# Last batch of a fused attention and mixture kernel: GpSimd in written order, w2's blocks in other buffers, one low part on VectorE

## The chip, the cores and the metric

The kernel runs on one core of one Trainium2 chip. The metric is device time in microseconds (us) of one execution, the median of several runs. Engines: PE is TensorE, DVE is VectorE, ACT is ScalarE, POOL is GpSimd, SP is SyncE, which here only issues DMAs.

## The reference, cut to what matters

Attention over 4 batches of 768 rows, 8 heads of 64; its output x, 3072 rows of 512, goes through four experts, all of which every row uses, weighted by its probabilities:

```python
p = domain_probs / (domain_probs.sum(-1, keepdims=True) + 1e-09)
out = np.zeros((N, D), dtype=np.float32)              # N = 3072, D = 512
for e in range(E):                                    # E = 4, F = 1024
    h = np.maximum(x @ w1[e], 0.0)
    out += p[:, e:e + 1] * (h @ w2[e])
```

## The kernel before

All is float32. To use TensorE's faster fp32r type without its error, an operand is split into a high part (the value rounded to fp32r, a copy by ScalarE or a cast by GpSimd) and a low part (value minus high part), and a product is three matmuls: high times high, low times high, high times low.

Batches 0 to 2 are interleaved with the attention of the next batch; the change leaves them alone. The last batch (`last_batch`) has no attention beside it. Its 16 units (4 experts, 4 groups of 256 hidden channels) are taken two by two, in eight stages j = 0 to 7. Both matrix products are done by a seven-product scheme for 2 by 2 blocks (Strassen's, in Winograd's form), so seven block products stand for eight.

In a unit (`small`), the seven products of w1's blocks with x's blocks (B11, T1, T2, B21, T3, T4, B22) are each 6 matmuls of 128x384, about 1.04 us. TensorE's order in a unit: A11·B11, S1·T1, S2·T2, A12·B21, S3·T3, A22·T4, S4·B22. S4·B22 is added onto the PSUM bank of S1·T1, so it can only begin when VectorE has read that bank (`ve.tensor_add(h22, pc[:, :HALF], u3)`, in the trace `hB<-pm,vv`). VectorE applies relu and the expert's share, which gives the hidden blocks `hb` B11, B22, B21, B12 (in the order they come).

At the end of a stage `sums` makes T3, T2, T1, T4 of the stage's hidden blocks on VectorE, and `form` splits all seven into `form` tiles, high part by ScalarE. The low parts of B11, B22 and B21 are GpSimd's (`po`), those of T3, T2, T1, T4 VectorE's.

In the next stage the seven big products (`big`, n = 0 to 6: A11·B11, A12·B21, S4·B22, S3·T3, S2·T2, S1·T1, A22·T4, each 12 matmuls, about 2.08 us) multiply these with the blocks of w2, in three places of the first unit and four of the second, the last of them (n = 6) just before S4·B22 of the second unit.

w2's blocks: A11, A12 and A22 come split from DRAM (`kept`). S1 to S4 are sums, made new in each stage: `ask_raw` loads 1 MB of w2 into one tile (named `x` in the trace, since it lies in the pool of that name), `sum_raw` makes the four sums in place on GpSimd (`x<-x`, four operations), and `ask` lets GpSimd cast each (high) and subtract (low) into a block buffer. That tile exists once: the next load waits until the last low part has been read from it, and the sums wait for the load.

Buffers: `wp` has two `w2s` tiles, each of two blocks, `L.w2f` three of one block. Before, one `w2s` holds A11 and A12, the other S4 and S3; S2, S1 and A22 take the `w2f` tiles. The last stage (j = 7) makes plain hidden parts instead of `form` tiles; for it `load_w2` loads two whole w2 tiles (1 MB each) into the two `w2s` buffers, and a last product for t = 0 to 5 ends the kernel.

What sets the order: each engine runs one queue in the order the scheduler wrote. In the last batch nothing is held in program order, so the scheduler may move instructions on every engine. DMAs of SP stand in one queue: one whose buffer is not free holds up those behind it.

Of the kernel before, what the change touches and what calls it, by code (L numbers as in the profile page):

```python
# [10 lines left out]
F32R = mybir.dt.float32r  # L11
# [3 lines left out]
ALU = mybir.AluOpType  # L15
# [3 lines left out]
P = 128  # L19
# [6 lines left out]
def f32(ap):  # L26
    return ap.bitcast(F32)
# [159 lines left out]
def attn_moe_kernel(ctx: ExitStack, tc, q, k, v, n_global, n_local, domain_probs, w1, w2, out):  # L187
# [19 lines left out]
    ve, ac, po, sy, te = (Ordered(tc, e) for e in (nc.vector, nc.scalar, nc.gpsimd, nc.sync, nc.tensor))  # L207
# [62 lines left out]
    wp = main.enter_context(tc.tile_pool(name="wp", bufs=2))  # L270
# [485 lines left out]
    kept, waiting = {}, {}  # L756
# [209 lines left out]
    def last_batch(L):  # L966

        b = LAST
        hb = {n: L.hb.tile([P, 2, HALF], F32, name=f"h{n}") for n in ("B11", "B12", "B21", "B22")}
        made, acc, share, w2f = {}, {}, {}, {}  # L970

        def form(name, src, low):
            t = made[name] = L.form.tile([P, 2, 2, HALF], F32R, name="form")
            ac.copy(t[:, 0], src)
            low.tensor_tensor(t[:, 1], src, f32(t[:, 0]), op=ALU.subtract)

        def sums():
            t3 = L.hb.tile([P, 2, HALF], F32, name="hT3")
# [9 lines left out]
        ORDER2 = (("A11", "B11"), ("A12", "B21"), ("S4", "B22"), ("S3", "T3"), ("S2", "T2"), ("S1", "T1"), ("A22", "T4"))  # L988
# [5 lines left out]
        a11, a21, a12, a22 = (raw[:, :, f, m] for f in range(2) for m in range(2))  # L994
        value = {"S1": a22, "S2": a11, "S3": a21, "S4": a12}

        def ask_raw(j):
            if j < per // 2 - 1:
                e, g = divmod(j, NPR // 2)
                for u in range(2):  # L1000
                    rows = w2[e, (2 * g + u) * 2 * P : (2 * g + u + 1) * 2 * P, :]
                    sy.dma_start(
                        raw[:, u].rearrange("p f m c -> p f (m c)"), rows.rearrange("(f p) m -> p f m", p=P)
                    )

        def sum_raw(j):
            if j < per // 2 - 1:
                po.tensor_add(a22, a21, a22)
                po.tensor_sub(a21, a11, a21)
                po.tensor_sub(a11, a22, a11)  # L1010
                po.tensor_sub(a12, a12, a11)

        def ask(j, n):
            if j >= per // 2 - 1:
                return
            e, g = divmod(j, NPR // 2)
            a = ORDER2[n][0]
            if n < 4:
                if n % 2 == 0:
                    w2f[(j, n // 2)] = wp.tile([P, 2, 2, 2, 2 * P], F32R, name="w2s")  # L1020
                t = w2f[(j, a)] = w2f[(j, n // 2)][:, n % 2]
            else:
                t = w2f[(j, a)] = L.w2f.tile([P, 2, 2, 2 * P], F32R, name="w2f")
            if a in value:
                po.tensor_copy(t[:, :, 0], value[a])
                po.tensor_tensor(t[:, :, 1], value[a], f32(t[:, :, 0]), op=ALU.subtract)
                if n == 5:
                    ask_raw(j + 1)
            else:
                f, m = {"A11": (0, 0), "A12": (1, 0), "A22": (1, 1)}[a]  # L1030
                for u in range(2):
                    block = kept[(e, 2 * g + u, 2)][:, :, f, m * 2 * P : (m + 1) * 2 * P]
                    sy.dma_start(f32(t[:, u]), f32(block))

        def big(j, n):
            a, x = ORDER2[n]
            pm = L.pq.tile([P, 2, 512], F32, name="pq")
            w, t = w2f[(j, a)], made[x]
            for m in range(2):
                at = 0  # L1040
                for u in range(2):
                    for wi, xi in ((0, 0), (1, 0), (0, 1)):
                        te.matmul(
                            pm[:, m, :HALF], w[:, u, wi, m * P : (m + 1) * P], t[:, xi, u, :],
                            start=(at == 0), stop=(at == 5),
                        )
                        at += 1
            if j == 0:
                acc[x] = L.acc.tile([P, 2, HALF], F32, name=f"sum{x}")
                ac.copy(acc[x], pm[:, :, :HALF])  # L1050
            else:
                ve.tensor_add(acc[x], pm[:, :, :HALF], acc[x])
            if n > 3:
                ask(j + 1, n)
            elif n % 2 == 1:
                ask(j + 1, n - 1)
                ask(j + 1, n)

        def small(i, more, plain=None):

            u = i % 2

            def out(name, f, c, src):
                if plain is None:
                    ve.scalar_tensor_tensor(
                        hb[name][:, u], src, 0.0, share[i][:, c * HALF : (c + 1) * HALF], op0=ALU.max, op1=ALU.mult
                    )
                else:
                    h = plain[f]
                    ac.activation(h[:, 0, c], src, AF.Relu)  # L1070
                    ve.scalar_tensor_tensor(h[:, 1, c], src, 0.0, f32(h[:, 0, c]), op0=ALU.max, op1=ALU.subtract)

            keep(i, 1)
            pa = product(i, "A11", "B11")
            p1 = up1.tile([P, HALF], F32, name="p1")
            ac.copy(p1, pa[:, :HALF])
            yield
            pc = product(i, "S1", "T1")
            yield
            more()  # L1080
            product(i, "S2", "T2", pm=pa, onto=True)
            u2 = up.tile([P, HALF], F32, name="u")
            ac.copy(u2, pa[:, :HALF])
            yield
            pd = product(i, "A12", "B21")
            ve.tensor_add(pd[:, :HALF], pd[:, :HALF], p1)
            out("B11", 0, 0, pd[:, :HALF])
            if u == 1 and plain is None:
                form("B11", hb["B11"], po)
            yield  # L1090
            more()
            product(i, "S3", "T3", pm=pa, onto=True)
            u3 = up.tile([P, HALF], F32, name="vv")
            ac.copy(u3, pa[:, :HALF])
            yield
            h22 = hb["B22"][:, u]
            ve.tensor_add(h22, pc[:, :HALF], u3)
            out("B22", 1, 1, h22)
            if u == 1 and plain is None:
                form("B22", hb["B22"], po)  # L1100
            more()
            product(i, "A22", "T4", pm=pa, onto=True)
            out("B21", 1, 0, pa[:, :HALF])
            if u == 1 and plain is None:
                form("B21", hb["B21"], po)
            yield
            if u == 1:
                more()
            product(i, "S4", "B22", pm=pc, onto=True)
            ve.tensor_add(pc[:, :HALF], pc[:, :HALF], u2)  # L1110
            out("B12", 0, 1, pc[:, :HALF])
            yield

        final = {}
        for j in range(per // 2):
            e, g = divmod(j, NPR // 2)
            if g == 0:
                pb = L.share.tile([P, S], F32, name="share")
                sy.dma_start(
                    pb.rearrange("p (t c) -> p t c", c=P),  # L1120
                    shares["all"][b * NQT : (b + 1) * NQT, e].partition_broadcast(P),
                )
            at = [0]

            def more():
                if j > 0:
                    big(j - 1, at[0])
                    at[0] += 1

            if j == 0:  # L1130
                ask_raw(0)
                sum_raw(0)
                for n in range(7):
                    ask(0, n)
            for i in (b * per + 2 * j, b * per + 2 * j + 1):
                share[i] = pb
                plain = None
                if j == per // 2 - 1:
                    plain = final[i] = [L.form.tile([P, 2, 2, HALF], F32R, name="form") for _ in range(2)]
                chores.append(load_w1(i + 2))  # L1140
                if j == per // 2 - 1:
                    chores.append(load_w2(i))
                for _ in small(i, more, plain):
                    work_chores()
                    yield
            if j < per // 2 - 1:
                sums()
                sum_raw(j + 1)


        for to, other in (("T2", "B11"), ("T3", "T2"), ("B21", "B11"), ("T4", "T3"), ("T2", "T1"), ("B22", "T2"), ("T1", "T3")):
# [45 lines left out]
    def work_chores():  # L1197
        for c in list(chores):
            if next(c, 0) == 0:
                chores.remove(c)  # L1200
# [49 lines left out]
    op = early.enter_context(tc.tile_pool(name="op", bufs=1))  # L1250
# [14 lines left out]
    per = E * NPR  # L1265
# [34 lines left out]
    L = Pools(main, "last", dict(form=7, acc=1, w2f=3, hb=1, share=2), dict(pq=2))  # L1300
    for _ in last_batch(L):
        pass
# [34 lines left out]
```

## Time and profile before

| | us |
|---|---|
| median of 3 runs | 1233.14 (1231.83 to 1234.08) |
| the profiled execution, its own time | 1231.64 |
| its span, first to last instruction | 1229.9 |
| busy in the span: PE, DVE, ACT, POOL | 1174.1, 842.3, 516.2, 339.5 |

Times below are from the span's start; the last batch begins at about 942. A line of the timeline gives start, length, engine, operation, output<-inputs, how many were merged, and in brackets the engine's idle time before it and who ended it. The seven forms of hidden blocks all are `form`, hidden blocks all `hB`. A digit of the granted clock in 40 slices is that of 30.7 us, in tenths of full speed.

### The profile page before, as it was taken

Reading aid. Unit: us, or ns where it says so; the run is one execution under the profiler, and the core shown is the slowest. Engines: PE = TensorE matmul, PEld = TensorE weight load, DVE = VectorE, ACT = ScalarE, POOL = GpSimd, SP = SyncE. Lnnn points to the kernel's source line nnn. Section 1 sums busy time; section 2 is a strip of 40 time slices with the busy share of each in tenths; the row PEclk is TensorE's granted clock in tenths of the full one; section 3 lists DMA queues with packets and bytes.
Section 4 is the critical chain, followed back from the end, with each engine's and each line's share of the span. In section 5 each row is a group of like instructions: output and inputs, shape, how many; then the busy total and the mean of one; then the engine's idle time right before and its main releaser. Section 6 shows DMA issues by size and latency. Waiting matters only on the chain.

```text
span 1229.9 us, 18538 instructions
## 1 busy us (share of the span) xinstructions
PE 1174.1 (95%) x6849; PEld 1066.7 (87%) x6849; DVE 842.3 (68%) x1699; ACT 516.2 (42%) x1296; POOL 339.5 (28%) x317
## 2 busy tenths in 40 slices
PE   8989999999999999999999999999999598888898
PEld 6778888889889989989989998998988498888897
DVE  6977676666677676677677757666757457777774
ACT  5735656555533434354432434444432242222231
POOL 5744736363620000000010000000003565555530
PEclk8999999999999999999999999999999799999999
DMA  9377787886988875867658666766545465455541
GB/s 194 66 240 233 258 257 256 274 280 208 338 310 249 258 222 168 246 195 204 206 180 282 208 191 210 199 221 199 175 175 197 156 213 173 149 200 205 205 146 54
DMA packets 162722, 258.29 MB, mean 210 GB/s; under 512 B 109024, under 2 KB 131136, under 8 KB 148032
## 3 DMA queue, kind: packets, MB, share of 16 engines
q1 hardware_dynamic: 159024, 250.74, 64.5%
q10 hardware_dynamic: 3600, 6.29, 1.4%
q8 instruction: 56, 0.92, 0.3%
q14 instruction: 42, 0.34, 0.1%
HBM read 185.65 MB, written 52.48 MB: 194 GB/s over the span
## 4 chain that ended last, share of the span: by engine, by line
PE 78%; DVE 8%; DMA 6%; POOL 4%; issue 2%; ACT 2%; SPq 1%; POOLq 0%; DVEq 0%; ACTq 0%
PE pm L42 62%; PE pt L42 6%; PE pq L42 6%; PE ps L42 4%; DVE form L42 2%; DMA raw<-in_moe_w_dram 2%; DVE hB L42 2%; DMA qd<-st_q 1%; DMA x<-in_moe_w_dram 1%; POOL w1s L42 1%; DVE pm L42 1%; DMA w1s<-kept 1%; POOL sums L42 1%; POOL w2f L42 1%; SPq L42 1%
## 5 line engine op out<-in xcount | busy, mean ns | idle before, releaser
L42 PE MATMUL pm<-w2s,h 128*128 128x512 f32 x1728 | 418.0, 394 | 3.2 <-DVE h L42 3.2
L42 PEld LDWEIGHTS pm<-w2s,h 128*128 128x128 f32 x1728 | 318.2, 188 | 70.3 <-DVE h L42 5.3
L42 PE MATMUL pm<-xT,w1s 128*128 128x384 f32 x1536 | 304.6, 339 | 4.0 <-DVE h L42 1.1
L42 DVE SCALAR_TENSOR_TENSOR acc<-pm,prob,acc 128x512 f32<-128x512 f32 x270 | 200.7, 748 | 114.1 <-PE pm L42 112.3
L42 PEld LDWEIGHTS pm<-xT,w1s 128*128 128x128 f32 x1536 | 268.0, 189 | 8.1 <-DVE h L42 2.2
L42 PE MATMUL pm<-xB,w1s 128*128 128x384 f32 x1152 | 235.1, 347 | 18.2 <-DVE hB L42 18.2
L42 PEld LDWEIGHTS pm<-xB,w1s 128*128 128x128 f32 x1152 | 207.4, 194 | 23.2 <-DVE hB L42 20.0
L42 POOL TENSOR_TENSOR xT<-x,xT 128x768 fp32r<-128x768 f32 x3 | 5.6, 1856 | 577.8 <-ACT xT L42 577.8
L42 ACT ACTIVATE h<-pm 128x384 fp32r<-128x384 f32 x192 | 92.3, 490 | 91.8 <-DVE pm L42 87.2
L42 ACT ACTIVATE pb<-pb,nmax 128x256 f32<-128x256 f32 (+1 forms) x192 | 92.9, 486 | 85.6 <-DVE nmax L42 85.0
L42 DVE SCALAR_TENSOR_TENSOR h<-pm,h 128x384 fp32r<-128x384 f32 x192 | 104.9, 551 | 12.1 <-ACT h L42 10.0
L42 ACT COPY p<-pm 128x384 f32<-128x384 f32 x64 | 30.5, 477 | 192.4 <-PE pm L42 175.5
L42 PE MATMUL pq<-form,w2s 128*128 128x384 f32 x336 | 64.3, 339 | 14.2 <-POOL form L42 14.2
L42 PEld LDWEIGHTS pq<-form,w2s 128*128 128x128 f32 x336 | 59.7, 191 | 14.6 <-POOL form L42 14.6
L42 ACT ACTIVATE pb<-pb,zsum 128x256 f32<-128x256 f32 (+1 forms) x144 | 63.0, 484 | 22.2 <-DVE zsum L42 22.1
L42 ACT COPY pT<-pt 128x512 f32<-128x512 f32 (+2 forms) x73 | 39.9, 547 | 49.0 <-PE pt L42 48.6
L42 DVE CUSTOM_DVE_ANT_0 pb<-ps,nbias 128x256 f32<-128x256 f32 (+1 forms) x144 | 52.9, 395 | 9.6 <-PE pt L42 6.0
L42 DVE TENSOR_TENSOR u<-pm,p 128x384 f32<-128x384 f32 x48 | 26.7, 556 | 46.9 <-PE pm L42 35.3
L42 POOL TENSOR_TENSOR x<-x 128x512 f32<-128x512 f32 x28 | 45.1, 1612 | 43.3 <-DMA x<-in_moe_w_dram 41.7
L42 PE MATMUL pt<-ident,pb 128*128 128x128 f32 x352 | 55.0, 277 | 1.7 <-DVE pT L42 1.0
L42 POOL TENSOR_TENSOR w2s<-raw,w2s 128x512 fp32r<-128x512 f32 x32 | 41.7, 1320 | 50.7 <-ACT w2s L42 50.6
L42 DVE TENSOR_TENSOR pm<-pm,vv 128x384 f32<-128x384 f32 x96 | 53.7, 559 | 2.7 <-PE pm L42 2.4
(146 smaller groups left out, 1461.2 us busy)
## 6 DMA issues: line engine op xcount, KB each, us to landing
w1s<-kept SPq DMA_DIRECT2D x48, 1792.0 KB, 7.8
w2s<-kept SPq DMA_DIRECT2D x34, 1024.0 KB, 5.1
kept<-w1s SPq DMA_DIRECT2D x16, 1792.0 KB, 10.0
qd<-st_q SPq DMA_DIRECT2D x96, 192.0 KB, 4.0
raw<-in_moe_w_dram SPq DMA_DIRECT2D x32, 512.0 KB, 6.0
kept<-w2s SPq DMA_DIRECT2D x16, 1024.0 KB, 8.2
w2s<-kept SPq DMA_DIRECT2D x28, 256.0 KB, 4.5
x<-in_moe_w_dram SPq DMA_DIRECT2D x14, 512.0 KB, 4.7
```

The source lines that it names most:

```text
L42: ins = fn(*args, **kwargs)
```

## The change

Three things, all in `last_batch`. GpSimd's instructions (sums, casts, low parts) are given to `keep_in_program_order`, so that the scheduler leaves them in the order of the program, and that order is changed: the sums of stage j's raw tile now stand in the first unit of stage j, behind its A12·B21, no longer at the end of the stage before, and each block is asked for after its own big product. The blocks share buffers otherwise: one `w2s` has A11 and A12 as before, the other S1 and A22; S4, S3 and S2 take the three `w2f` tiles. The raw tile of the next stage is asked for behind the last of the seven (n = 6). The low part of B21 goes from GpSimd to VectorE.

```diff
+            if low is po:
+                keeping(ins)
...
-                po.tensor_add(a22, a21, a22)
+                keeping(po.tensor_add(a22, a21, a22))
...
         def ask(j, n):
-            if j >= per // 2 - 1:
+
+            if j >= per // 2 - 1 or n in (0, 5):
                 return
             e, g = divmod(j, NPR // 2)
-            a = ORDER2[n][0]
-            if n < 4:
-                if n % 2 == 0:
-                    w2f[(j, n // 2)] = wp.tile([P, 2, 2, 2, 2 * P], F32R, name="w2s")
-                t = w2f[(j, a)] = w2f[(j, n // 2)][:, n % 2]
+            names = {1: ("A11", "A12"), 2: ("S4",), 3: ("S3",), 4: ("S2",), 6: ("S1", "A22")}[n]
+            if len(names) == 2:
+                t = wp.tile([P, 2, 2, 2, 2 * P], F32R, name="w2s")
             else:
-                t = w2f[(j, a)] = L.w2f.tile([P, 2, 2, 2 * P], F32R, name="w2f")
...
+                    keeping(po.tensor_copy(to[:, :, 0], value[a]))
+                    keeping(po.tensor_tensor(to[:, :, 1], value[a], f32(to[:, :, 0]), op=ALU.subtract))
...
+            if n == 6:
+                ask_raw(j + 1)
...
-            if n > 3:
-                ask(j + 1, n)
-            elif n % 2 == 1:
-                ask(j + 1, n - 1)
-                ask(j + 1, n)
+            ask(j + 1, n)
...
             out("B11", 0, 0, pd[:, :HALF])
+            if u == 0 and i > b * per:
+                sum_raw((i - b * per) // 2)
...
-                form("B21", hb["B21"], po)
+                form("B21", hb["B21"], ve)
...
                 sums()
-                sum_raw(j + 1)
```

The first place: GpSimd's queue where the last batch begins. `x_9982` is the raw tile; `w2s_9996` and the tiles numbered near it are stage 0's blocks. Before:

```order
L42 TENSOR_TENSOR w2f_10004<-x_9982,w2f_10004 128x2x256
L42 TENSOR_TENSOR x_9982<-x_9982 128x2x256 x4
L42 TENSOR_TENSOR form_10107<-hB11_9978,form_10107 128x768
L42 TENSOR_TENSOR form_10120<-hB22_9981,form_10120 128x768
L42 TENSOR_TENSOR form_10130<-hB21_9980,form_10130 128x768
L42 CAST w2s_10305<-x_9982 128x2x256 x2
```

Now:

```order
L42 TENSOR_TENSOR w2s_10005<-x_9982,w2s_10005 128x2x256
L42 TENSOR_TENSOR form_10107<-hB11_9978,form_10107 128x768
L42 TENSOR_TENSOR form_10120<-hB22_9981,form_10120 128x768
L42 TENSOR_TENSOR x_9982<-x_9982 128x2x256 x4
L42 CAST w2f_10257<-x_9982 128x2x256
```

The low parts of stage 0's hidden B11 and B22 moved ahead of the four sums of stage 1's raw tile; that of B21 left this queue.

The second place: the end of stage 2 and the change to stage 3, one period of what repeats. GpSimd before (`w2f_10618` is S2, `w2f_10648` S1):

```order
L42 CAST w2f_10618<-x_9982 128x2x256
L42 TENSOR_TENSOR form_10601<-hB11_9978,form_10601 128x768
L42 TENSOR_TENSOR w2f_10618<-x_9982,w2f_10618 128x2x256
L42 CAST w2f_10648<-x_9982 128x2x256
L42 TENSOR_TENSOR form_10631<-hB22_9981,form_10631 128x768
L42 TENSOR_TENSOR w2f_10648<-x_9982,w2f_10648 128x2x256
L42 TENSOR_TENSOR form_10660<-hB21_9980,form_10660 128x768
L42 TENSOR_TENSOR x_9982<-x_9982 128x2x256 x4
```

Now (`w2f_10619` is S2, `w2s_10673` S1 and A22):

```order
L42 TENSOR_TENSOR form_10602<-hB11_9978,form_10602 128x768
L42 CAST w2f_10619<-x_9982 128x2x256
L42 TENSOR_TENSOR w2f_10619<-x_9982,w2f_10619 128x2x256
L42 TENSOR_TENSOR form_10632<-hB22_9981,form_10632 128x768
L42 CAST w2s_10673<-x_9982 128x2x256
L42 TENSOR_TENSOR w2s_10673<-x_9982,w2s_10673 128x2x256
L42 TENSOR_TENSOR x_9982<-x_9982 128x2x256 x4
```

The cast of S1 moved behind the low part of B22 and now writes a buffer that big product n = 6 of the stage reads; the low part of B21 left the queue, so nothing stands between S1's low part and the sums of the next raw tile.

The same change of stage in SP's queue, before (`w1s` are w1's blocks for the unit after next, `w2f_10677` is A22):

```order
L42 DMA x_9982<-in_moe_w2_dram 128x2x512 x2
L42 DMA w1s_10556<-kept_1_3_1_2385 128x3584
L42 DMA w2f_10677<-kept_1_0_2_2124 128x2x256
L42 DMA w2f_10677<-kept_1_1_2_2298 128x2x256
L42 DMA w2s_10772<-kept_1_2_2_2524 128x2x256
```

Now:

```order
L42 DMA w2s_10673<-kept_1_0_2_2124 128x2x256
L42 DMA w2s_10673<-kept_1_1_2_2298 128x2x256
L42 DMA w1s_10559<-kept_1_3_1_2385 128x3584
L42 DMA x_9982<-in_moe_w2_dram 128x2x512 x2
L42 DMA w2s_10772<-kept_1_2_2_2524 128x2x256
```

The raw load went from ahead of A22 and of a `w1s` load to behind both.

The third place: TensorE's last products, where `w2s_11794` and `w2s_11902` are the two whole w2 tiles. Before:

```order
L42 MATMUL pq_11990<-form_11780,w2f_11755 128x384 x12
L42 MATMUL pm_11904<-xB22_9829,w1s_11636 128x384 x6
L42 MATMUL pm_12021<-w2s_11794,form_11783 128x512 x3
L42 MATMUL pm_12021<-w2s_11794,form_11784 128x512 x3
L42 MATMUL pm_12021<-w2s_11902,form_11891 128x512 x3
```

Now:

```order
L42 MATMUL pq_11990<-form_11780,w2s_11753 128x384 x12
L42 MATMUL pm_11904<-xB22_9829,w1s_11639 128x384 x6
L42 MATMUL pm_12021<-w2s_11794,form_11783 128x512 x3
L42 MATMUL pm_12021<-w2s_11794,form_11784 128x512 x3
L42 MATMUL pm_12034<-w2s_11794,form_11783 128x512 x3
L42 MATMUL pm_12034<-w2s_11794,form_11784 128x512 x3
L42 MATMUL pq_12047<-ident_58,sumB21_10225 128x128 x2
L42 MATMUL pq_12047<-ident_58,sumT4_10400 128x128 x2
L42 MATMUL pq_12053<-ident_58,sumB21_10225 128x128 x2
L42 MATMUL pq_12053<-ident_58,sumT4_10400 128x128 x2
L42 MATMUL pm_12063<-w2s_11794,form_11783 128x512 x2
L42 MATMUL pm_12021<-w2s_11902,form_11891 128x512 x3
```

Twelve matmuls on the first tile, eight transposes and two matmuls more now stand ahead of the first use of `w2s_11902`; before, only six matmuls did.

## Rows read from the trace of the kernel before

**Rows 1.** The page: busy time by engine, and the granted TensorE clock in 40 slices.

```profile
PE 1174.1 (95%) x6849; PEld 1066.7 (87%) x6849; DVE 842.3 (68%) x1699; ACT 516.2 (42%) x1296; POOL 339.5 (28%) x317
...
PEclk8999999999999999999999999999999799999999
```

**Rows 2.** Who TensorE waited for, from 930 to the end: total us, times, longest.

```profile
PE pm L42 <- DVE hB L42: 18.2, 5, 3.8
PE pq L42 <- POOL form L42: 14.2, 1, 14.2
```

**Rows 3.** Timeline of TensorE where stage 1 begins (big n = 0, A11·B11, then S2·T2).

```profile
957.38 0.51 PE L42 MATMUL pq<-form,w2s 128*128 128x384 f32 x2
972.14 2.61 PE L42 MATMUL pq<-form,w2s 128*128 128x384 f32 x7 [14.25 <-POOL form L42]
974.55 1.89 PE L42 MATMUL pm<-xB,w1s 128*128 128x384 f32 x6
...
977.86 1.20 PE L42 MATMUL pm<-xT,w1s 128*128 128x384 f32 x6
```

**Rows 4.** Timeline of GpSimd in the same place.

```profile
946.58 4.23 POOL L42 TENSOR_TENSOR x<-x 128x512 f32<-128x512 f32 x3 [18.26 <-DMA x<-in_moe_w_dram]
...
958.44 1.26 POOL L42 TENSOR_TENSOR w2f<-x,w2f 128x512 fp32r<-128x512 f32 x1
965.05 5.28 POOL L42 TENSOR_TENSOR x<-x 128x512 f32<-128x512 f32 x4 [5.35 <-DMA x<-in_moe_w_dram]
970.29 6.07 POOL L42 TENSOR_TENSOR form<-hB,form 128x768 fp32r<-128x768 f32 x3
```

**Rows 5.** The chain of waits: start, length, what. Where stage 1 begins, the first of two w1s loads issued behind the raw load, to its landing; near the end, the eight transposes of the first two output tiles.

```profile
960.72 8.48 DMA w1s<-kept
...
1210.55 0.87 PE pq L42 x8
```

**Rows 6.** Timeline of TensorE: the change from stage 2 to stage 3 (big n = 6, then S4·B22 with stage 3's A11·B11), and the restarts of the first unit's S4·B22 after the waits in stage 3 and in stage 6 (the second and the last of five).

```profile
1034.23 2.24 PE L42 MATMUL pq<-form,w2f 128*128 128x384 f32 x12
1036.31 2.24 PE L42 MATMUL pm<-xB,w1s 128*128 128x384 f32 x12
...
1053.81 3.65 PE L42 MATMUL pm<-xB,w1s 128*128 128x384 f32 x12 [3.81 <-DVE hB L42]
...
1157.49 3.66 PE L42 MATMUL pm<-xB,w1s 128*128 128x384 f32 x12 [3.68 <-DVE hB L42]
```

**Rows 7.** Timeline of TensorE in stage 7, which has no raw tile: S4·B22 of stage 6 with A11·B11; A22·T4 and S4·B22 of the first unit; S4·B22 of the second; the last product.

```profile
1174.51 2.24 PE L42 MATMUL pm<-xB,w1s 128*128 128x384 f32 x12
...
1186.99 1.21 PE L42 MATMUL pm<-xT,w1s 128*128 128x384 f32 x6
1188.12 2.38 PE L42 MATMUL pm<-xB,w1s 128*128 128x384 f32 x12
...
1203.86 1.20 PE L42 MATMUL pm<-xB,w1s 128*128 128x384 f32 x6
1204.90 5.65 PE L42 MATMUL pm<-w2s,form 128*128 128x512 f32 x24
```

**Rows 8.** Timeline of VectorE at the change to stage 3: the last sum of big products, the hidden block B12 from PSUM, T3, the low parts of T2, T1 and T4, and the add that reads the bank of S1·T1.

```profile
1036.51 0.96 DVE L42 TENSOR_TENSOR sumT<-pq,sumT 128x768 f32<-128x768 f32 x1 [1.52 <-PE pq L42]
...
1038.15 0.56 DVE L42 SCALAR_TENSOR_TENSOR hB<-pm,share 128x384 f32<-128x384 f32 x1
1038.74 1.79 DVE L42 TENSOR_TENSOR hT<-hB,hB 128x768 f32<-128x768 f32 x1
...
1045.54 5.96 DVE L42 TENSOR_TENSOR form<-hB,form 128x768 fp32r<-128x768 f32 x3
...
1053.21 0.54 DVE L42 TENSOR_TENSOR hB<-pm,vv 128x384 f32<-128x384 f32 x1
```

**Rows 9.** Timeline of VectorE at the change to stage 7: the same three low parts and the same add.

```profile
1183.12 2.69 DVE L42 TENSOR_TENSOR form<-hB,form 128x768 fp32r<-128x768 f32 x3
...
1187.52 0.55 DVE L42 TENSOR_TENSOR hB<-pm,vv 128x384 f32<-128x384 f32 x1
```

**Rows 10.** Timeline of GpSimd at the change to stage 3: cast S1, low B22, low S1, low B21, sums.

```profile
1034.24 0.60 POOL L42 CAST w2f<-x 128x512 fp32r<-128x512 f32 x1
1034.82 1.84 POOL L42 TENSOR_TENSOR form<-hB,form 128x768 fp32r<-128x768 f32 x1
1036.62 1.29 POOL L42 TENSOR_TENSOR w2f<-x,w2f 128x512 fp32r<-128x512 f32 x1
1037.88 1.84 POOL L42 TENSOR_TENSOR form<-hB,form 128x768 fp32r<-128x768 f32 x1
1043.50 7.18 POOL L42 TENSOR_TENSOR x<-x 128x512 f32<-128x512 f32 x4 [3.78 <-DMA x<-in_moe_w_dram]
```

**Rows 11.** Timeline of ScalarE in the same place: the high part of B21.

```profile
1035.02 0.84 ACT L42 CAST form<-hB 128x768 fp32r<-128x768 f32 x1 [0.96 <-DVE hB L42]
```

**Rows 12.** DMA issues in short windows, KB each and median us from issue to landing: the raw load issued at 1037.94, the w1s load issued behind it at 1038.92, a w1s load issued alone at 1055.57.

```profile
x<-in_moe_w_dram SPq DMA_DIRECT2D x2, 512.0 KB, 4.5
...
w1s<-kept SPq DMA_DIRECT2D x1, 1792.0 KB, 8.8
...
w1s<-kept SPq DMA_DIRECT2D x1, 1792.0 KB, 7.4
```

**Rows 13.** The two loads of whole w2 tiles in stage 7, issued at 1184.1 and 1193.7, with nothing but each other on the queue for the second.

```profile
DMA to landing us min/median/max: 5.0/5.8/6.6
```

More of the change, by code (lines that the diff above doesn't have):

```diff
@@ L970, in last_batch @@
         made, acc, share, w2f = {}, {}, {}, {}
+        keeping = tc.keep_in_program_order
         def form(name, src, low):
@@ L974, in form @@
             ac.copy(t[:, 0], src)
-            low.tensor_tensor(t[:, 1], src, f32(t[:, 0]), op=ALU.subtract)
+            ins = low.tensor_tensor(t[:, 1], src, f32(t[:, 0]), op=ALU.subtract)
+            if low is po:
+                keeping(ins)
         def sums():
@@ L1007, in sum_raw @@
             if j < per // 2 - 1:
-                po.tensor_add(a22, a21, a22)
-                po.tensor_sub(a21, a11, a21)
-                po.tensor_sub(a11, a22, a11)
-                po.tensor_sub(a12, a12, a11)
+                keeping(po.tensor_add(a22, a21, a22))
+                keeping(po.tensor_sub(a21, a11, a21))
+                keeping(po.tensor_sub(a11, a22, a11))
+                keeping(po.tensor_sub(a12, a12, a11))
         def ask(j, n):
-            if j >= per // 2 - 1:
+            if j >= per // 2 - 1 or n in (0, 5):
@@ L1015, in ask @@
                 return
             e, g = divmod(j, NPR // 2)
-            a = ORDER2[n][0]
-            if n < 4:
-                if n % 2 == 0:
-                    w2f[(j, n // 2)] = wp.tile([P, 2, 2, 2, 2 * P], F32R, name="w2s")
-                t = w2f[(j, a)] = w2f[(j, n // 2)][:, n % 2]
-            else:
-                t = w2f[(j, a)] = L.w2f.tile([P, 2, 2, 2 * P], F32R, name="w2f")
[L1024 to L1033, printed above, removed]
+            names = {1: ("A11", "A12"), 2: ("S4",), 3: ("S3",), 4: ("S2",), 6: ("S1", "A22")}[n]
@@ new lines, in ask @@
+            if len(names) == 2:
+                t = wp.tile([P, 2, 2, 2, 2 * P], F32R, name="w2s")
+            else:
+                t = L.w2f.tile([P, 1, 2, 2, 2 * P], F32R, name="w2f")
+            for at, a in enumerate(names):
+                to = w2f[(j, a)] = t[:, at]
+                if a in value:
+                    keeping(po.tensor_copy(to[:, :, 0], value[a]))
+                    keeping(po.tensor_tensor(to[:, :, 1], value[a], f32(to[:, :, 0]), op=ALU.subtract))
+                else:
+                    f, m = {"A11": (0, 0), "A12": (1, 0), "A22": (1, 1)}[a]
+                    for u in range(2):
+                        block = kept[(e, 2 * g + u, 2)][:, :, f, m * 2 * P : (m + 1) * 2 * P]
+                        sy.dma_start(f32(to[:, u]), f32(block))
```

## The prediction

> **What bounds the kernel now.** I read the page first. TensorE is busy 95% of the span, so only its idle time and its slow clock can be won; one slice of 40 has a granted clock of 0.7, the one where the last batch begins [rows 1]. Then the view of who waited for whom, over the last batch: TensorE waits for little more than two things, once 14.2 us for a low part of GpSimd and five times, 18.2 us in all, for a hidden block of VectorE [rows 2]. The timelines tell why.
>
> The long wait: big product n = 0 of stage 1 issues two matmuls at 957.4 and goes on at 972.14 [rows 3]. It needs the low part of B11. GpSimd is done with stage 0's blocks at 959.70, but next in its queue are the sums of stage 1's raw tile, whose load has not landed; they run from 965.05, and the low part comes from 970.29 to about 972.1 [rows 4].
>
> The five short waits, here in stage 3: count from T0, the end of S4·B22 that closes a stage. Rows 6 put it at 1037.35 (half of the twelve matmuls from 1036.31; twelve take 36.31 - 34.23 = 2.08 us, one 0.173). TensorE next waits from T0+12.65 to T0+16.46 for the add that reads the bank of S1·T1 [rows 6]. VectorE makes that add from T0+15.86 [rows 8], late because its three low parts took 5.96 us and T3 1.79. While they ran, GpSimd did the sums (7.18 us from 1043.50) and the low part of B21 (to 1039.72) [rows 10]. Stage 7 shows it without sums: the three low parts take 2.69, the add comes at T0+11.97 with T0 = 1175.55, and S4·B22 follows 0.1 us behind A22·T4 [rows 7, 9]. So the wait is there when GpSimd's sums lie on VectorE's low parts, and nearly gone when not.
>
> What a wait costs with its slow restart: from the restart in stage 3 to that in stage 6 are three periods, (1157.49 - 1053.81)/3 = 34.56 us [rows 6]. Stage 7, from S4·B22 to S4·B22, takes 1203.86 - 1174.51 = 29.35 [rows 7]. The difference is 5.21 a stage, 3.64 of it the idle time, the rest the restart: its twelve matmuls take 3.65 us [rows 6] where they take 2.24 otherwise [rows 7].
>
> **The written order at the start.** GpSimd's work up to 959.70 is the same (four sums, four casts, four low parts); the low part of B11 now follows it at once, 959.7 to 961.6 or, if VectorE's new low part of B21 comes between, about 1 us later. Big n = 0 then goes on some 10.5 us sooner. But what is late next is w1's blocks for A11·B11: their load stands in SP's queue behind the raw load, which waits for GpSimd's last low part both before and now; it is issued at 960.72 and lands 8.48 us later, at 969.2 [rows 5]. So A11·B11 starts at about 969.25 in place of 974.55 [rows 3], 5.3 sooner. Both runs restart slowly there: before, the nine matmuls of big n = 0 bore most of it, now A11·B11 and S1·T1 do. From 972.14 to 977.86 TensorE did 7 + 6 + 6 + 3 = 22 matmuls in 5.72 us against 3.81 at 0.173; the 15 behind A11·B11's start would need 2.6 + 1.9 = 4.5, so S2·T2 starts at 973.75 in place of 977.86: **4.1 us** won. Bounds: nothing, if the queue moves for another reason; 10.5 plus 1.9, if w1's blocks came in time.
>
> **The buffers and the raw load.** The load still waits for the low part of S1, but S1's cast now waits until big n = 6 has been read, T0-1.04. Cast 0.60 and low part 1.29 [rows 10] end at T0+0.9, and the load is issued at T0+1.0 to T0+1.6, against T0+0.6 before (1037.94) [rows 12]. In SP's queue it is now behind A22 and behind a w1s load issued at about T0+0.2. This decides whether the sums still lie on VectorE's low parts, which end at T0+10.26 in stage 7 (1183.12 + 2.69) [rows 9]. The lower bound is 4.5 us from issue as now [rows 12]: T0+5.6. The upper is w1s alone, 7.4, and the full 4.5 behind it: T0+12.1. I take the upper half: a w1s load with the raw load ahead lands 8.8 after issue, 1.4 later than alone although it was issued 1.0 later [rows 12], so loads of this queue share little and pass one after another, and the raw tile's own transfer is about 2.4 us. That gives T0+7.6+2.4 = T0+10.0, and A22's 0.5 MB ahead adds up to 1.2. The sums then run from T0+10 to T0+11 on, beside adds that read PSUM, which GpSimd does not hold up: B12's operation of 0.56 at 1038.15 lies wholly beside the low part of B21 [rows 8, 10].
>
> The five waits are gone with that: 5 x 5.21 = **26.0 us**, of which the small wait of stage 7 is kept in, since 29.35 includes it. Later sums harm nobody: from T0+16 GpSimd has the casts and low parts of S4 and S3 (1.9 each) to do before the low part of B11, whose product ends at T0+19.8 (eleven of 1.04, four of 2.08) and which TensorE needs at T0+31.
>
> **B21's low part on VectorE** adds 0.95 us (an operation of its size in rows 8 takes 0.96) seven times. Its high part ends at 1035.86, T0-1.5 [rows 11], and VectorE is idle for 1.52 us up to 1036.51 [rows 8], so most of it lies in idle time. What follows it on VectorE is the last sum, the add for B12, B12 and then T3. T3 took 1.79 beside GpSimd's low part of B21, which is gone, and 0.83 with it. The bounds: 0.83 won, if B21's stays in the gap; 2.1 lost a stage, if GpSimd's low B22, cast S1 and low S1 each go ahead of it: then it runs T0+1.2 to T0+2.2, behind it 0.96 + 0.6 + 0.6 + 0.96 for sum, add, B12 and T3, which ends at T0+5.3 in place of T0+3.18. I take a delay of about 0.5, which the shorter T3 pays, and 0.1 a stage for what is left: **-0.5 us**.
>
> Here the profile shows that T3 with 0.98 us of GpSimd's low part beside it takes 0.83 longer than an operation of its size [rows 8, 10]. The Trainium skill, page "SBUF — State Buffer", section "Who interferes with whom", says that a VectorE instruction with two SBUF inputs and a GpSimd instruction that reads SBUF exclude each other, whole instruction by whole instruction. The trace agrees. It speaks against this third edit, since the low part of B21 has two SBUF inputs and now runs where GpSimd has low B22, cast S1 and low S1 in a row.
>
> **The end.** The second whole w2 tile now goes into the buffer of S1 and A22, free when the last big product is done at 1203.86, not at 1193.7. By the second of the two loads, 5.0 us [rows 13], it lands at 1208.9. Ahead of its first use stand now 12 + 2 matmuls of 0.235 (5.65 for 24) [rows 7] and eight transposes, 0.87 [rows 5]: 1204.90 + 3.3 + 0.9 = 1209.1. So no wait, or by the other load, 6.6, one of 1.5: **-0.3 us**.
>
> **Sum.** 4.1 + 26.0 - 0.5 - 0.3 = 29.3 of the profiled execution's 1231.64 leaves 1202.3. The median of the runs is 1.5 above it: 1203.8, and I say **1204**.
>
> **Rivals.**
> 1. Part of the waits stays: the raw tile lands at T0+8.5 to T0+9.5, and one or two of the three low parts wait for an operation of the sums (1.1 each, 5.96 - 2.69 over three). For it: 10.0 is an estimate with an issue time uncertain by 0.6. Against it: A22 ahead only delays. Waits of 0.6 to 1.7, with up to 1.6 of slow restart, five times: 3 to 16 us less is won, 1207 to 1220, say 1211.
> 2. The sums stay on the low parts, as the lower bound has it, T0+5.6. Then the low parts take 3.3 longer again, less 0.5 from T3: 2.8 + 1.6 against 5.21, 0.8 a stage won: 4 + 4.1 - 0.3 = 7.8, 1225. The Trainium skill speaks for it: "DMA: Bandwidth & Descriptors", section "Queues, rings and completion order", says that loads of one issuing engine need not complete in the order of issue. The rows on the w1s load speak against it, as above.
> 3. Slower than before: VectorE is locked out at the stage change. Place: B21's low part loses each time to GpSimd's low B22, cast S1 and low S1, so T3 ends 2.1 later, and the sums lie on the low parts as in rival 2. The wait is 3.64 + 2.1 + 1.6 = 7.3 against 5.21, 10.5 us lost over five stages, less 4.1 - 0.3 at start and end: 1240. It decides from a delay of 0.8 a stage with the sums where they were. Alone, without the sums, it would still be 1222. Against it: low B22 ends at T0-0.7 and S1's cast cannot start before T0-1.04, so one turn at least is VectorE's.
> 4. Better: w1's blocks come in time at the start, 8 us more, 1196.
>
> **Chances.** The forecast 0.66, its own range 1200 to 1207; rival 1 0.18; rival 2 0.08, of which 0.03 is no change; rival 3 0.05; rival 4 0.03. The range from 1197 to 1218 leaves out the dearer end of rival 1, rivals 2 and 3 and half of 4, under 0.2. About 0.2% (2.5 us) is what a measurement can tell from no change. Faster 0.66 + 0.18 + 0.05 + 0.03 = 0.92, no change 0.03, slower 0.05.
>
> **What would show it.** Right: TensorE's wait for GpSimd's low part at the start shrinks to some 4 us, with one for a w1s load behind it; periods from S4·B22 to S4·B22 of about 29.4 in stages 2 to 6; VectorE's three low parts at about 2.7; sums that start at T0+10 or later; T3 at about 0.95. Wrong: sums that start before T0+9, low parts near 6, or a new wait of TensorE for `w2s` at the end of more than 1.5.

## The result, and the profile after

The changed kernel takes 1203.51 us in the median (1201.47 to 1206.03, four runs); the kernel before, beside it on the same chip, 1232.84 (1231.83 to 1234.08). The ratio is 0.976, 95% interval 0.974 to 0.9785: 29.3 us won. The profiled execution took 1204.6 us, its span is 1202.8.

The page, busy time by engine and the granted TensorE clock in 40 slices, answers to [rows 1]:

```profile
PE 1167.6 (97%) x6849; PEld 1059.5 (88%) x6849; DVE 827.3 (69%) x1706; ACT 515.8 (43%) x1296; POOL 324.9 (27%) x310
...
PEclk8999999999999999999999999999999979999999
```

The number of matmuls is the same, VectorE has seven instructions more, GpSimd seven fewer: B21's low parts. GpSimd is busy 14.6 us less, of which the seven low parts, 1.84 each, are 12.9; VectorE is busy 15.0 us less although it has more to do, so it was held up less. The slice with a granted clock of 0.7, where stage 1 begins, is still there. Who TensorE waited for, from 930 to the end, answers to [rows 2]:

```profile
PE pq L42 <- POOL form L42: 7.0, 1, 7.0
PE pm L42 <- DMA w1s<-kept: 4.5, 1, 4.5
```

VectorE's five waits are gone; the long wait for GpSimd has halved, and a wait for w1's blocks is new. Timelines show both places. First the change from stage 2 to stage 3, on TensorE: S4·B22 that closes stage 2 (with stage 3's A11·B11), S1·T1, and S4·B22 of the first unit, where the wait was [rows 6]:

```profile
1030.44 2.24 PE L42 MATMUL pm<-xB,w1s 128*128 128x384 f32 x12
1032.52 1.20 PE L42 MATMUL pm<-xT,w1s 128*128 128x384 f32 x6
...
1043.96 2.24 PE L42 MATMUL pm<-xB,w1s 128*128 128x384 f32 x12
```

VectorE there: B21's low part, T3, the three low parts, and the add that frees the bank [rows 8]:

```profile
1030.08 1.24 DVE L42 TENSOR_TENSOR form<-hB,form 128x768 fp32r<-128x768 f32 x1 [0.96 <-ACT form L42]
...
1033.28 0.96 DVE L42 TENSOR_TENSOR hT<-hB,hB 128x768 f32<-128x768 f32 x1
...
1038.62 2.69 DVE L42 TENSOR_TENSOR form<-hB,form 128x768 fp32r<-128x768 f32 x3
...
1043.02 0.55 DVE L42 TENSOR_TENSOR hB<-pm,vv 128x384 f32<-128x384 f32 x1
```

GpSimd there: low B22, cast S1, low S1, sums [rows 10]:

```profile
1028.65 1.84 POOL L42 TENSOR_TENSOR form<-hB,form 128x768 fp32r<-128x768 f32 x1
1030.67 1.12 POOL L42 CAST w2s<-x 128x512 fp32r<-128x512 f32 x1 [0.17 <-PE pq L42]
1031.87 1.30 POOL L42 TENSOR_TENSOR w2s<-x,w2s 128x512 fp32r<-128x512 f32 x1
1044.51 5.65 POOL L42 TENSOR_TENSOR x<-x 128x512 f32<-128x512 f32 x4 [11.35 <-DMA x<-in_moe_w_dram]
```

T0, the end of S4·B22, is read as the start of S1·T1 behind it less 1.04: 1031.48. The low parts take 2.69 (before 5.96), T3 0.96 (before 1.79), and the sums run only from T0+13.0, when the add that TensorE needs is already done. S4·B22 of the first unit follows A22·T4 with no wait and no slow restart.

Why the sums are late is to be seen in SP's queue at the same stage change, A22's two halves, w1s, and the two halves of the raw load:

```profile
1030.63 1.19 SPq L42 DMA_DIRECT2D w2s<-kept  x2
1031.91 0.56 SPq L42 DMA_DIRECT2D w1s<-kept  x1
1033.19 1.33 SPq L42 DMA_DIRECT2D x<-in_moe_w_dram  x2
```

and in the times from issue to landing, here of the first stage change (KB each, median us), which answer to [rows 12]:

```profile
w1s<-kept SPq DMA_DIRECT2D x1, 1792.0 KB, 9.8
...
x<-in_moe_w_dram SPq DMA_DIRECT2D x2, 512.0 KB, 10.4
```

The raw load is issued when the low part of S1 is done (1031.87 + 1.30 = 1033.17), behind w1s, and lands 10.3 us later (10.4 at the first stage change) instead of 4.5.

Where stage 1 begins, TensorE now reads as follows, against [rows 3]:

```profile
958.74 0.51 PE L42 MATMUL pq<-form,w2s 128*128 128x384 f32 x2
966.21 2.61 PE L42 MATMUL pq<-form,w2s 128*128 128x384 f32 x7 [6.96 <-POOL form L42]
973.31 2.29 PE L42 MATMUL pm<-xB,w1s 128*128 128x384 f32 x6 [4.49 <-DMA w1s<-kept]
...
977.39 1.21 PE L42 MATMUL pm<-xT,w1s 128*128 128x384 f32 x6
```

The start won little: S2·T2 stands at 977.39, before at 977.86. From there to the start of S1·T1 in stage 7 it is 1149.57 - 977.39 = 172.18 us, before 1176.59 - 977.86 = 198.73. So 0.5 us were won at the start and 26.55 in the five stage changes; the spans differ by 27.1, which leaves nothing for the end.

### The profile page after: what moved, and what is told of

It reads as the page before. It is cut to its first block, busy times and chain, and to the rows that moved or that the text cites. A ratio compares the mean times of both kernels' runs of the same rounds, so it can differ in the third digit from the quotient of the medians.

```text
span 1202.8 us, 18559 instructions
## 1 busy us (share of the span) xinstructions
PE 1167.6 (97%) x6849; PEld 1059.5 (88%) x6849; DVE 827.3 (69%) x1706; ACT 515.8 (43%) x1296; POOL 324.9 (27%) x310
## 4 chain that ended last, share of the span: by engine, by line
PE 83%; DMA 6%; DVE 4%; POOL 3%; ACT 2%; issue 1%; SPq 1%; POOLq 0%; DVEq 0%; ACTq 0%
PE pm L42 65%; PE pq L42 8%; PE pt L42 6%; PE ps L42 4%; DMA raw<-in_moe_w_dram 2%; DMA qd<-st_q 1%; DMA x<-in_moe_w_dram 1%; POOL w1s L42 1%; DMA w1s<-kept 1%; POOL sums L42 1%; SPq L42 1%; DMA q<-in_q_dram 1%; POOL w2s L42 1%; DMA w2s<-kept 1%; POOL w2f L42 0%
## 5 line engine op out<-in xcount | busy, mean ns | idle before, releaser
L42 PE MATMUL pm<-xB,w1s 128*128 128x384 f32 x1152 | 228.8, 340 | 4.6 <-DMA w1s<-kept 4.5
L42 PEld LDWEIGHTS pm<-xB,w1s 128*128 128x128 f32 x1152 | 201.6, 189 | 8.9 <-DMA w1s<-kept 5.0
L42 ACT COPY p<-pm 128x384 f32<-128x384 f32 x64 | 30.6, 478 | 168.0 <-PE pm L42 149.4
L42 POOL TENSOR_TENSOR x<-x 128x512 f32<-128x512 f32 x28 | 37.1, 1327 | 79.0 <-DMA x<-in_moe_w_dram 57.5
```

Source lines behind the costliest of these rows:

```text
L42: ins = fn(*args, **kwargs)
```

## The experiments

The theory: the raw load's new place, behind w1s, brings GpSimd's sums clear of VectorE's three low parts, and this alone ends the five waits. Its rivals: B21's move, GpSimd's written order, or the buffers. At the start the theory was that w1s is the next to be late. Each run below was timed beside the kernel before, whose median was 1231.95 to 1234.23 there; ratios are to it, with 95% intervals. Two medians from different runs are compared by these intervals, and what is said of a single place in the kernel comes from one trace of each kernel.

**B21's low part back on GpSimd.**

```diff
-                form("B21", hb["B21"], ve)
+                form("B21", hb["B21"], po)
```

> The changed kernel with one part undone: the low part of B21 is GpSimd's again (one instruction of 128x768 a stage goes back from VectorE to GpSimd). Theory (the five waits went because the raw load stands behind A22 and w1s in SP's queue and its sums so come clear of VectorE's three low parts): the waits stay gone, the time is 1202 to 1208 us, and the sums still start 11 us or more after T0. Rival (the waits went because GpSimd was freed of B21's low part): most of the 26 us comes back, 1215 to 1230 us, with PE waiting for VectorE's hB again.

Measured: 1206.57 us, 0.978 (0.975 to 0.981). As the theory has it: the sums start at T0+13.1, the low parts take 2.69, the waits for hB sum to 0.2 us.

**GpSimd's order left to the scheduler.**

```diff
-        keeping = tc.keep_in_program_order
+        keeping = lambda ins: ins
```

> The changed kernel without the written order of GpSimd's work; the buffers and VectorE's B21 stay. Theory: the order in which GpSimd works is not what ends the five waits, so they stay gone; only the first of the seven stages may lose 0 to 5 us since casts of w2's blocks come ahead of the two low parts that A11.B11 waits for there: 1203 to 1209 us. Rival (the written order is what keeps the sums off VectorE's low parts): the waits come back, 1215 to 1232 us.

Measured: 1206.45 us, 0.978 (0.974 to 0.981). No wait for hB, and the five stage changes take 145.8 us, in the changed kernel 146.2. At the start the wait for GpSimd's low part is long again, and the one for w1s is gone:

```profile
PE pq L42 <- POOL form L42: 15.4, 1, 15.4
```

Counted from the first product of stage 0, S2·T2 of stage 1 comes after 38.9 us, in the changed kernel after 35.4, before after 36.15. The written order therefore acts at the start alone. There it is worth 3.5 us by the traces: it takes 8.4 us off the wait for GpSimd (15.4 to 7.0), and the new wait for w1s takes back 4.5. Without it the start is 2.7 us longer than before, so something else in the change costs time there, or the first raw tile landed later; no run tells which.

**The raw load ahead of w1s again**, by issuing w1s's load in `small` behind the last `more()` and holding it there:

```diff
+                if 0 < j < per // 2 - 1:
+                    for _ in load_w1(i + 2, pin=True):
+                        pass
...
-                chores.append(load_w1(i + 2))
+                if not (i % 2 == 1 and 0 < j < per // 2 - 1):
+                    chores.append(load_w1(i + 2))
```

> The changed kernel with one thing moved: in the five stage changes the raw load is issued ahead of w1s in SP's queue, as in the kernel before; all else stays, GpSimd's order and VectorE's B21 among it. Theory: the raw block lands about 6 to 7 us after T0, its sums lie beside VectorE's three low parts again, those take 5 us and more instead of 2.7, and PE waits 2.5 to 5 us a stage for hB: 1216 to 1230 us. Rival (the place of the raw load doesn't matter, the freed GpSimd or its order did it): 1202 to 1205 us, no wait.

Measured: 1209.67 us, 0.9815 (0.978 to 0.985). Waits and slow low parts are back, so the rival falls, but at 6 us, half the price that the theory set at the least. The first stage change, T0 = 999.53, by its timelines: SP's raw load and w1s, GpSimd's sums, VectorE's low parts, and the wait:

```profile
1001.06 0.90 SPq L42 DMA_DIRECT2D x<-in_moe_w_dram  x2
1002.06 0.42 SPq L42 DMA_DIRECT2D w1s<-kept  x1
```

```profile
1006.99 6.65 POOL L42 TENSOR_TENSOR x<-x 128x512 f32<-128x512 f32 x4 [5.95 <-DMA x<-in_moe_w_dram]
```

```profile
1006.27 4.88 DVE L42 TENSOR_TENSOR form<-hB,form 128x768 fp32r<-128x768 f32 x3
```

```profile
1013.46 2.35 PE L42 MATMUL pm<-xB,w1s 128*128 128x384 f32 x12 [1.28 <-DVE hB L42]
```

The low parts began 0.7 us before the sums, so the first of the three was already running: 0.9 for it and 2.0 for each of the others give 4.9. TensorE's wait is 1.3 to 1.5 us, and behind it twelve matmuls take 2.35 to 2.38, not 3.65: the granted clock from 1010 to 1150 is 1.00, before it was 0.95.

**The kernel before, with only the raw load moved behind w1s.**

```diff
-                    sy.dma_start(
+                    ins = sy.dma_start(
...
+                    if j > 1:
+                        tc.keep_in_program_order(ins)
```

> The kernel before with one thing moved: the raw load of the stages from the second on stands behind the second w1s load (and the loads of w2 ahead of it) in SP's queue; buffers, GpSimd's order and B21 as before. Theory: this alone takes the five waits away, 26 us less, 1205 to 1209 us. Rival (the buffers or VectorE's B21 are needed as well): 1222 to 1234 us.

Measured: 1206.66 us, 0.979 (0.9755 to 0.982). This is the main proof: old buffers, old order, B21 on GpSimd, and the waits for hB are 0.2 us in all. SP's w1s and raw load, GpSimd's sums and VectorE's low parts in the first stage change, whose T0 is 1003.75:

```profile
1004.19 0.55 SPq L42 DMA_DIRECT2D w1s<-kept  x1
1004.83 0.90 SPq L42 DMA_DIRECT2D x<-in_moe_w_dram  x2
```

```profile
1017.00 5.84 POOL L42 TENSOR_TENSOR x<-x 128x512 f32<-128x512 f32 x4 [10.89 <-DMA x<-in_moe_w_dram]
```

```profile
1011.32 2.69 DVE L42 TENSOR_TENSOR form<-hB,form 128x768 fp32r<-128x768 f32 x3
```

**The kernel before, with only B21's low part moved** (`po` to `ve` in its `form` line).

> The kernel before with one part of the change alone: the low part of B21 on VectorE; buffers, GpSimd's order and the raw load ahead of w1s as before. Theory after the first four runs (VectorE's three low parts begin some 1.2 us earlier after T0 where B21 is VectorE's, so that less of them lies beside the sums: 4.88 us instead of 5.96 with the raw load first): the five waits shrink from 3.5 to 1.5 us and the clock holds behind them, 3.5 us a stage, 1213 to 1218 us. Rival (the step from 3.5 to 1.5 came from the buffers or from GpSimd's order): 1228 to 1234 us.

Measured: 1228.08 us, 0.996 (0.994 to 0.998). A miss of the theory by some 10 us, at the rival's edge; the edit is worth about 5 us here (3 to 7 by the interval). The low parts do begin 1.2 us sooner (T0+6.7 instead of T0+7.9), but here the sums begin at T0+6.5 and still cover all three, which take 5.98. TensorE's first two waits, from its timeline:

```profile
1019.83 2.35 PE L42 MATMUL pm<-xB,w1s 128*128 128x384 f32 x12 [2.38 <-DVE hB L42]
...
1052.30 3.29 PE L42 MATMUL pm<-xB,w1s 128*128 128x384 f32 x12 [3.08 <-DVE hB L42]
```

**Both undone: raw load first and B21 on GpSimd**, in the changed kernel (the two diffs above together).

> The changed kernel with two parts undone together: the raw load ahead of w1s in SP's queue and the low part of B21 on GpSimd; the buffers and GpSimd's written order stay. Theory (each of VectorE's three low parts takes 2.0 us beside the sums and 0.9 us clear of them; with B21 on GpSimd they begin 1.0 us later after T0, so all three lie beside): low parts 5.9 to 6.0 us, five waits of 3 to 4 us with a clock that falls behind them, 1226 to 1234 us. Rival (B21's engine and the load's place add up, 3 us for the one and 6 for the other): 1211 to 1215 us.

Measured: 1219.85 us, 0.989 (0.9865 to 0.991), between the two. The low parts begin 1.0 us later as expected, at T0+7.76, but the raw load does too: it waits for the low part of S1, and GpSimd has B21's low part to do first. The sums begin at T0+7.92, the low parts again take 4.88, the waits are 2.3 us each. GpSimd's sums and VectorE's low parts, with T0 = 998.59:

```profile
1006.51 7.18 POOL L42 TENSOR_TENSOR x<-x 128x512 f32<-128x512 f32 x4 [5.37 <-DMA x<-in_moe_w_dram]
```

```profile
1006.35 4.88 DVE L42 TENSOR_TENSOR form<-hB,form 128x768 fp32r<-128x768 f32 x3
```

What I had left out is that B21's low part stands ahead of both, of the sums and of VectorE's low parts.

**The raw load first, but no sums.** In the five stage changes the four sums are left out, so that S1 to S4 are there made of unsummed blocks; the load and its place stay as in the run with the raw load ahead.

```diff
-            if j < per // 2 - 1:
+            if j < 1:
                 keeping(po.tensor_add(a22, a21, a22))
```

> The changed kernel with the raw load ahead of w1s, and GpSimd's four sums of the raw block left out in the five stage changes (so S1 to S4 of those stages are made of blocks that aren't summed); the load, its bytes and its place stay. Theory (it is the sums, GpSimd reading beside VectorE, that slow the three low parts): low parts 2.7 us again, no wait for hB, 1200 to 1204 us. Rival (it is the 1 MB raw load landing beside them): low parts still 4.9 us, waits of 1.5 us, 1207 to 1211 us.

Measured: 1201.80 us, 0.974 (0.972 to 0.976). The load is issued at T0+1.5, as in the run with the raw load ahead; the low parts take 2.69, there is no wait for hB. The raw load and the low parts, with T0 = 1002.58:

```profile
1004.11 0.91 SPq L42 DMA_DIRECT2D x<-in_moe_w_dram  x2
```

```profile
1009.31 2.69 DVE L42 TENSOR_TENSOR form<-hB,form 128x768 fp32r<-128x768 f32 x3
```

It is the sums that slow VectorE, not the transfer. The Trainium skill, page "SBUF — State Buffer", section "Who interferes with whom", says that a VectorE instruction with two SBUF inputs contends with a GpSimd instruction that reads SBUF; this pair of runs agrees and has the price: 4.88 us with sums, 2.69 without.

All runs on the stage change in one table, in us: T0+ is for the first of the five changes, "five" is from T0 there to T0 of stage 7.

| kernel | low parts begin | sums begin | low parts | waits for hB, sum | five | median |
|---|---|---|---|---|---|---|
| before | T0+7.9 | T0+5.9 | 5.96 | 18.2 | 172.7 | 1232.84 |
| before, B21 on VectorE | T0+6.7 | T0+6.5 | 5.98 | 14.7 | 168.0 | 1228.08 |
| after, raw first, B21 on GpSimd | T0+7.8 | T0+7.9 | 4.88 | 11.6 | 164.9 | 1219.85 |
| after, raw first | T0+6.7 | T0+7.5 | 4.88 | 7.3 | 154.4 | 1209.67 |
| before, raw behind w1s | T0+7.6 | T0+13.3 | 2.69 | 0.2 | 147.2 | 1206.66 |
| after, B21 on GpSimd | T0+7.8 | T0+13.1 | 2.69 | 0.2 | 147.8 | 1206.57 |
| after, GpSimd's order free | T0+6.7 | T0+13.0 | 2.69 | none | 145.8 | 1206.45 |
| after | T0+6.7 | T0+13.0 | 2.69 | none | 146.2 | 1203.51 |
| after, raw first, no sums | T0+6.7 | never | 2.69 | none | 145.7 | 1201.80 |

Moved behind w1s, the raw load does it alone (172.7 to 147.2). Moved back in the changed kernel, it costs 8.2 of the 26.6 us alone and 18.7 together with B21's low part: there the sums begin so late that two of the three low parts lie beside them, in the kernel before all three.

**The start: w1s ahead of the second raw load.** The load is asked for behind both w1s loads of stage 1 and held there.

```diff
-            if n == 6:
+            if n == 6 and j > 0:
                 ask_raw(j + 1)
...
+                    if i == b * per + 1 and k == 0:
+                        ask_raw(1)
```

> The changed kernel with one thing moved at the start of the last batch: the raw load of the second pair of blocks is issued behind the two w1s loads there, not ahead of them; these then needn't stand in SP's queue behind a load that waits for GpSimd's last read of the raw buffer at 963.7. Theory (the start won 0.5 us instead of 4.1 since w1s landed at 973.3): the 4.5-us wait for w1s goes, the 7.0-us wait for GpSimd's low part stays, 1198 to 1201 us. Rival (GpSimd's chain alone sets the start and w1s only shows up behind it): another wait of the same end takes its place, 1202 to 1206 us.

Measured: 1193.63 us, 0.9665 (0.964 to 0.969): 9.9 us under the changed kernel by the medians, about twice what was expected. Whom TensorE waited for at the start:

```profile
PE pq L42 <- POOL form L42: 4.9, 1, 4.9
```

The wait for w1s is gone, and the one for GpSimd is 2.1 us shorter although GpSimd is no sooner. The reason is in TensorE's queue: the scheduler, with w1s no longer late, put A11·B11 and S1·T1 of the next unit ahead of the matmuls that need the low part. TensorE's queue there in the changed kernel and in this one:

```diff
-L42 MATMUL pq<-form,w2s 128x384 x9
+L42 MATMUL pq<-form,w2s 128x384 x2
 L42 MATMUL pm<-xB_9827,w1s 128x384 x6
 L42 MATMUL pm<-xT_9855,w1s 128x384 x6
-L42 MATMUL pq<-form,w2s 128x384 x3
+L42 MATMUL pq<-form,w2s 128x384 x10
```

From the first product of stage 0 to S2·T2 of stage 1 it is 27.6 us here, 35.4 in the changed kernel, 36.15 before. How much of the 7.8 is due to w1s and how much to the two products that now fill the wait was not told apart. The two spans differ by 8.9 us, and 2.0 of these lie ahead of the last batch, which the edit leaves alone.

**The start: B11's low part on VectorE**, in the first stage only (in `form` of B11, `ve if i == b * per + 1 else po`).

> The changed kernel with the low part of B11 of the first stage of the last batch on VectorE (one instruction of 128x768). Theory (w1s sets when the start ends): PE's 7.0-us wait for GpSimd shrinks to under 1 us, the wait for w1s grows from 4.5 to about 10 us as w1s lands where it did, and the time is 1201 to 1205 us. Rival (GpSimd's low part sets it): the 7.0 us are won, 1196 to 1198 us.

Measured: 1201.95 us, 0.974 (0.972 to 0.976). TensorE's waits:

```profile
PE pm L42 <- DMA w1s<-kept: 9.8, 1, 9.8
PE pq L42 <- DVE form L42: 0.6, 1, 0.6
```

As the theory has it, 7.0 us for GpSimd become 0.6, and 4.5 for w1s become 9.8. A wait removed is here for the most part a wait moved. The size is in part luck: w1s did not land where it did, but 29.0 us after stage 0's first product instead of 31.3, since GpSimd's chain began 1.3 us sooner and ran 0.9 us shorter in this trace.

**Both at the start.**

> Both moves at the start of the last batch: w1s ahead of the raw load, and B11's low part of the first stage on VectorE. Theory (two waits of near the same end, GpSimd's and w1s's): together they win 9 to 12 us where each alone wins 0 to 5, 1191 to 1195 us. Rival (a third supplier ends as late, such as VectorE's hT or ScalarE's copies): 1196 to 1203 us.

Measured: 1192.10 us, 0.965 (0.962 to 0.968), the best of all runs and clear of the changed kernel's interval. In the last batch TensorE waits for neither GpSimd, w1s nor hB; the longest wait left is 1.3 us, for ScalarE. S2·T2 of stage 1 comes 20.8 us after stage 0's first product. Over w1s's move alone the gain, 1.5 us, is within the intervals.

## Why the prediction was right

It said 1204 us, from 1197 to 1218; 1203.51 was measured. The large term was right for the reason given, the start fell short by 3.6 us, and the other terms together came out 1.4 us better (26.55 in place of 25.2). That 1204 meets the median to 0.5 us is partly luck: the profiled executions, from which the sum was made, differ by 27.0 us and not by 29.3; the one before lay 1.5 below the median of its runs, the one after 1.1 above.

**The five waits, 26.0 won.** Right in size and in cause. From T0 of the first stage change to T0 of stage 7 the raw load's move alone, in the kernel before, wins 172.73 - 147.16 = 25.57. Two runs show the cause from both sides: the load moved alone in the kernel before does it, and moved back in the changed kernel undoes 8.2 us. The run without sums shows what it is of the load that matters. None of the rivals held: in the changed kernel the sums came at T0+12.9 or later in all five.

**When the raw tile lands.** Rightly late, but wrongly sized: I had T0+10.0 to T0+11.2, and the sums, which wait for it, began at T0+13.0, past my upper bound of T0+12.1. The raw load took 10.4 us from issue with w1s ahead, and w1s 9.8 with the raw load behind it, against 4.5 and 7.4 [rows 12]. The term that was too small is the 7.4 for w1s. It need not be the raw load that slows it: at the change to stage 7 of the kernel before, w1s stands behind A22 with no raw load near, the next load issued 8.1 us later, and lands 11.1 us after issue:

```profile
w1s<-kept SPq DMA_DIRECT2D x1, 1792.0 KB, 11.1
```

What A22 ahead does to w1s the sum had at 1.2 us at the most; no run tells it apart from the rest. That the raw tile lands behind w1s (T0+13.0 and T0+10.2) fits the step "pass one after another". Nothing hung on it: later sums harm nobody, as predicted, and no sums at all win only 0.4 us over the five stages.

**The place of the raw load, as I told it from the queue.** Right: A22, w1s, raw. The issue came at T0+1.7, where I had T0+1.0 to T0+1.6; S1's cast took 1.12, not 0.60, with VectorE's low part of B21 beside it.

**The start, 4.1 won.** This step failed in size: 0.5 was won, and the wait for GpSimd's low part was 7.0 us, not some 4. The mechanism held, the w1s load behind a raw load that waits for GpSimd, and w1s landing is what A11·B11 waits for. The sum took GpSimd's chain to run as before, up to 959.70. It did not, as GpSimd's timeline shows:

```profile
948.42 5.65 POOL L42 TENSOR_TENSOR x<-x 128x512 f32<-128x512 f32 x4 [19.78 <-DMA out_dram<-acc]
...
957.98 0.96 POOL L42 CAST w2f<-x 128x512 fp32r<-128x512 f32 x1
...
960.23 1.34 POOL L42 CAST w2s<-x 128x512 fp32r<-128x512 f32 x1
961.65 2.03 POOL L42 TENSOR_TENSOR w2s<-x,w2s 128x512 fp32r<-128x512 f32 x1
963.64 4.29 POOL L42 TENSOR_TENSOR form<-hB,form 128x768 fp32r<-128x768 f32 x2
```

It began 1.84 us later than in [rows 4], 0.27 of which is the batch's own later start, and took 15.3 us instead of 13.1 to the end of the last block. Most of the 2.1 us more are casts and a low part that take 0.6 and 1.3 elsewhere, here beside VectorE's work on the hidden blocks, B21's low part among it. So the raw load was issued 4.0 us later, at 963.71, and w1s landed as much later. The chain of waits has both loads, the first tile's raw load and the w1s load:

```profile
937.50 10.76 DMA x<-in_moe_w_dram
964.69 8.57 DMA w1s<-kept
```

In three kernels A11·B11, which waits for w1s, starts 9.5 to 9.9 us after that raw load is issued (963.71 to 973.31 here; 959.64 to 969.12 with B11 on VectorE; 959.30 to 969.15 with the raw load first in the stage changes). Before, w1s landed at 969.2, with the raw load issued at 959.73. From that issue to S2·T2 the sum had 14.0 us, and it was 13.7, 14.4 and 14.8 in these three. So the steps behind the issue were right, the time of the issue was wrong. Why the first raw tile lands later in some of the kernels is open: the median of its two halves was from 7.8 to 9.7 us over the twelve traces, with old and new buffers, and no run here tells what sets it.

**B21's low part on VectorE, 0.5 lost.** The wrong sign, by little. With it on GpSimd the five stage changes take 147.8, as changed 146.2: 0.3 a stage is won. The step that failed is that the delay on VectorE eats more than T3 gains. T3 takes 0.96 against 1.98 with B21 on GpSimd, and is done at T0+2.8, where it was at T0+3.2 before. The medians, 1206.57 and 1203.51, have overlapping intervals, so it is the traces that tell this. The rival that GpSimd locks VectorE out did not come: B21's low part took 1.24, a third over its own time. In the kernel before, where the sums lie on the low parts, the same edit was worth about 5 us.

**The end, 0.3 lost.** No wait for `w2s` came, as predicted, and nothing was lost: from S1·T1 of stage 7 to the end of the span it is 53.2 us, before 53.3.

## What to carry to other kernels

A transfer can be too early: if what consumes it holds up an engine on the critical path, its place in the issuing queue is a means to say when that consumer runs, and moving one load won 26 us in the kernel before with not an instruction less. Before taking a wait away, look up what lands next behind it: at the start GpSimd's low part came at 966.2 and w1s at 973.3, an edit to the first alone moved the wait to the second, and the load that was blocked in its queue behind a waiting load was the one worth moving. And where instructions of two engines hold each other up, ask which instruction stands ahead of both.

## What was not expected of the hardware

The price of the overlap is a step for each instruction: a VectorE low part of 128x768 takes 0.9 us clear of GpSimd's sums and 2.0 beside them (2.69 and 5.96 for three; 4.88 is one clear and two beside), so that a shift of 1 us in either is worth 1.1 us or nothing. In the five stage changes GpSimd's four sums took 5.4 to 5.8 us clear of the low parts and 6.6 to 8.0 beside them.

A wait's cost is not its length alone. Behind the five waits of 1.3 to 1.5 us no restart was slow (twelve matmuls in 2.35 to 2.38 us); behind those of 2.3 to 2.4 us in two kernels some were (3.85, 3.60, 3.75 and 3.09 us) and some were not (2.38 and 2.35), and behind all of 3.1 us and more they took 3.1 us or longer. The granted clock from 1010 to 1150 was 1.00 in the first case and 0.95 to 0.96 in the others.
